# A convolution-attention and feed-forward kernel on one core: both instruction lists in a new order, and a result bank opened by whichever unit comes first

## The chip, the core and the metric

The kernel runs on one core of a Trainium2 chip. The time is device microseconds of one execution, here the median of three runs. The engines named are TensorE (PE, matrix products), VectorE (DVE), ScalarE (ACT), GpSimd (POOL) and SyncE (SP, which issues the transfers). Each works through its own list of instructions strictly in order and waits where an instruction needs something that is not there yet.

## What is computed

A softmax over seven taps weighs seven shifted copies of `x`; the result goes through a feed-forward layer with a gate.

```
w = softmax(weight_gen, axis=-1)            # B=4, S=4096, H=8, K=7 taps
x_unf = x_pad[:, idx, :].reshape(B, S, K, H, 24)
x = einsum('bshk,bskhg->bshg', w, x_unf)    # -> 16384 tokens x 192
h = x @ w_in                                # 192 -> 2048
g = h * (1.0 / (1.0 + exp(-1.702 * h)))
out = g @ w_out                             # 2048 -> 192
```

## The kernel before

**Tiling.** The 16,384 tokens are cut into 32 blocks of 512, and the 2048 hidden columns into 16 groups of 128. One block with one group is a unit; there are 512. Block 0 is computed in fp32, the others in fp16 with each number split into a high and a low part, so that three products stand in for one.

**Per unit, from block 3 on.** `pair` (L661, `P.k` in the lists) makes the first products of two units in two banks, 18 matmuls on 64-row halves of the array. The gate of a unit is a tanh on ACT (L595, `gt`) and a multiply on DVE (L600, `gm`); then ACT writes the high part of `g` (L613, `gh`) and DVE the low part (L615, `gl`). Only `gl` frees the bank. Unit n uses bank h(n mod 4), so a pair waits for the `gl` of the two units two pairs earlier. `upper` (L677, `U.n`, six matmuls) adds the unit to 128 of the 192 output columns in two PSUM banks; `lower` (L690, `C.b`, 48 matmuls) does the remaining 64 columns for a whole block at once, and two small matmuls of a later block follow it (L351, `top`).

**Per block, the attention.** `softmax` has seven steps (`s`): maximum (DVE), subtraction (POOL L210), exp and sum, a small constant (ACT L220), reciprocal (DVE L222), multiply (POOL L228). `attend` then does seven taps (POOL L244) and six additions (POOL L260) on 128x768. `scales` takes the largest magnitude (DVE L369, L341, L346), spreads it with `top`, and makes powers of two of it (DVE L357 to L363); `cg` (L379) and `co` (L384) derive two more numbers from them. ACT then rounds the tile to its high part (L420, `x.0`), and DVE makes the low part in two instructions (L423, `x.1` with 128x512 and `x.2` with 128x256), both of whose inputs lie in SBUF. SP transposes the parts (L429, `tu`) and copies halves of them (L438/L441, `xd`); pairs need both. SP also loads weights and `x` for two blocks at a time (L199, L186, `lp`), and stores results after ACT and DVE have scaled them (`stU`, `stV`, `stLa`, `stLb`).

**What sets the order.** Every engine's order comes from two written lists of steps. `ORDER` has 923 items, for the start up to block 7 or so; `PERIOD` has 246, two blocks or 32 units, and is repeated with the block and unit numbers moved on by two blocks and 32 units. `act` walks them item by item, and each item issues its instructions on whatever engines it uses. No scheduler rearranges them. In a period the numbers are relative, so that `C.-1` is the `lower` of the block before (called the first place below) and `C.0` the next one's (the second place). Where the lists repeat, one period of the trace stands for all; the times below are from the one around 602 us.

**The start.** Block 0 is turned round by matmuls. Its columns beyond 128 (the rest) are built from seven partial products on POOL (L279), summed two by two (L314, `rests`) and transposed onto PE by L325 (`trb`). First products of block 0 are `W` and `X` (L567; L583, L584).

**Opening a bank.** In `upper` and `second` the first unit of a block, f = 0, allocates the result bank and sets `start`, and the last, f = 15, sets `stop`; so in the lists unit 0 is first and unit 15 last.

Of the kernel before, what the change touches and what calls it, by code (L numbers as in the profile page):

```python
# [22 lines left out]
P.0 a4.1 gh.-2 gm.-1 gl.-2 gh.-1 gl.-1 s1.2 U.-6 gt.0 a4p.1 P.1 gm.0 gt.1 gh.0 gm.1 gl.0 a5.1 U.-5 gt.2  # L23
stLb.-2 U.-4 gh.1 s0.3 gm.2 s2.2 U.-3 a5p.1 gl.1 gh.2 U.-2 s3.2 P.2 gl.2 s4.2 gt.3 a6.1 gm.3 co.-1 gh.3 s5.2
U.-1 gt.4 gl.3 a6p.1 U.0 stU.-1 gm.4 U.1 gt.5 stV.-1 P.3 s6.2 c0.1 a0.2 gm.5 C.-1 gt.6 a1.2 gh.4 gm.6 gt.7
gl.4 gh.5 gm.7 a1p.2 gh.6 gh.7 gl.6 gl.7 s1.3 gl.5 a2.2 P.4 c2.1 x0.1 a2p.2 s2.3 U.2 gt.8 P.5 x1.1 gt.9
stLa.-1 a3.2 gm.8 gh.8 gm.9 U.3 gh.9 U.4 x2.1 gt.10 a3p.2 gl.9 U.5 tu.1 gt.11 gl.8 U.6 gm.10 P.6 gh.10 gm.11
a4.2 gl.10 gh.11 gl.11 U.7 gt.12 a4p.2 U.8 gm.12 gt.13 xd.1 P.7 gh.12 gm.13 lp.4 gl.12 a5.2 co.0 cg.1
stLb.-1 U.9 gt.14 U.10 a5p.2 gh.13 gm.14 U.11 gl.13 gh.14 U.12 gt.15 P.8 a6.2 gm.15 gl.14 gh.15 s3.3 gl.15
a6p.2 U.13 gt.16 U.14 gm.16 gt.17 P.9 gh.16 gm.17 gl.16 gh.17 gl.17 U.15 gt.18 c0.2 P.10 stU.0 gt.19 stV.0  # L30
gm.18 U.16 gh.18 gm.19 C.0 gh.19 s4.3 gt.20 gm.20 gl.19 gh.20 gl.18 gt.21 gl.20 gm.21 gh.21 P.11 c2.2 stLa.0
# [12 lines left out]
nm.o2 n2.t1 s2.1 n1.o2 a1.4p nm.o4 W.8 na.i2w n2.o2 S.3 gm.6 gt.7 s3.1 s2.2 W.9 gm.7 a1.5 nm.o3 s2.3 S.4
n1.o3 s2.4 s3.2 na.i0w n2.o3 a1.5p X.2 s2.5 n1.o4 na.t0w s3.3 n2.o4 s2.6 bin.0 S.5 a1.6 gt.8 gt.9 gm.8
na.o2w gm.9 W.10 a1.6p s3.4 bin.1 W.12 gt.10 bin.2 na.o0w W.11 c1.0 a2.0 S.6 gt.11 nm.o5 gm.10 a2.1 ph.t0w
c1.1 W.13 c1.2 n1.o5 S.7 x1.0 pd.t0w a2.1p gm.11 n2.o5 X.3 na.o4w x1.1 a2.2 bout.0 S.8 gt.13 gt.12 s3.5
ph.i0w x1.2 bout.1 W.15 s3.6 gm.13 tu1 a2.2p bout.2 S.9 gt.15 gm.12 ph.o2w W.14 pl.i0w S.10 ph.o0w pl.t0w
ph.o4w xd1 W.16 pl.o2w S.11 gt.14 ps.o0w pl.o0w hold.B W.17 ph.i2w lp2 a2.3 gm.14 S.12 ps.o2w gm.15 cg1 X.4
pl.o4w S.13 gt.16 gt.17 a2.3p gm.16 W.18 gm.17 gh.16 gl.16 W.19 gt.18 a2.4 gh.17 W.20 gm.18 gt.19 gl.17  # L50
S.14b gh.18 gm.19 a2.4p S.14a gl.18 gh.19 W.21 co1 gl.19 S.15b a2.5 X.5 S.15a gt.21 pl.i2w W.22 st.0a gt.20
S.16a a2.5p gm.21 st.0b W.23 gm.20 gh.21 S.16b gh.20 gl.21 S.17a gt.22 a2.6 gl.20 S.17b gt.23 gm.22 W.24
gm.23 gh.22 a2.6p W.25 gh.23 gl.22 ps.o4w S.18 gl.23 s5.0 a3.0 c2.0 X.6 S.19 gt.24 gt.25 gm.24 W.27 a3.1
gm.25 gh.24 c2.1 S.20 c2.2 gh.25 gt.27 a3.1p gl.25 W.26 x2.0 s4.0 gm.27 S.21 gt.26 gl.24 a3.2 gh.27 W.29
gm.26 gh.26 S.22 x2.1 W.28 s4.1 cg2 gl.26 a3.2p s4.2 S.23 gl.27 X.7 S.24 gt.28 x2.2 a3.3 gt.29 tu2 gm.28
W.30 s4.3 gh.28 gm.29 S.25 gt.30 a3.3p co2 gm.30 W.31 gl.28 gh.30 S.26 gh.29 a3.4 gt.31 gl.29 xd2 mv W.32
gm.31 W.33 a3.4p gl.30 gh.31 S.27 gl.31 X.8 a3.5 S.28 gt.33 gt.32 gm.33 W.34 a3.5p s4.4 gm.32 gh.33 S.29
gh.32 gl.33 gt.34 s4.5 W.35 gl.32 a3.6 gm.34 S.30a gt.35 W.36 gh.34 gm.35 s4.6 S.30b gl.34 a3.6p gh.35 W.37
gl.35 S.31a X.9 c3.0 st.1a a4.0 S.31b gt.36 W.38 st.1b gm.36 gt.37 s5.1 S.32b gh.36 a4.1 gm.37 W.39 gt.38
gl.36 S.32a s5.2 gm.38 gh.37 S.33b a4.1p gh.38 c3.1 S.33a c3.2 gt.39 W.40 gl.37 x3.0 S.34 gm.39 a4.2 co3  # L60
gh.39 gl.38 W.41 s5.3 gl.39 a4.2p S.35 X.10 S.36 gt.41 x3.1 gt.40 a4.3 gm.41 W.43 gm.40 S.37 gt.43 x3.2
gh.41 W.42 a4.3p tu3 gh.40 S.38 gl.40 gt.42 gl.41 W.44 a4.4 gm.42 gm.43 S.39 gh.42 gh.43 gl.42 a4.4p W.45
s5.4 cg3 gl.43 xd3 S.40 a4.5 lp3 a4.5p X.11 S.41 gt.44 a4.6 gt.45 W.46 gm.45 S.42 gm.44 a4.6p gh.45 gt.46
gl.45 W.47 gh.44 gm.46 S.43 gl.44 gh.46 c4.0 gt.47 P.24 gm.47 s6.0 gl.46 S.44 gt.48 s7.0 gh.47 gm.48 c4.1
gt.49 S.45 gl.47 gh.48 gm.49 P.25 c4.2 gh.49 gl.48 x4.0 gl.49 U.48 gt.50 P.26 gm.50 gt.51 s5.5 gh.50 x4.1
s5.6 gm.51 S.46b S.46a gl.50 a5.0 gh.51 S.47b gt.52 gl.51 S.47a gt.53 gm.52 U.49 a5.1 st.2a gm.53 P.27 gh.52
gh.53 hold.A x4.2 gl.52 a5.1p tu4 U.50 gl.53 gt.54 U.51 cg4 gm.54 gt.55 P.28 a5.2 gh.54 gm.55 gh.55 st.2b
gl.55 a5.2p U.52 gt.56 gl.54 U.53 xd4 gt.57 gm.56 U.54 gh.56 gm.57 s6.1 P.29 gh.57 hold.C a5.3 gl.57 gl.56
U.55 gt.58 a5.3p P.30 gm.58 gt.59 gh.58 gm.59 gl.58 a5.4 gh.59 U.56 gt.60 gl.59 U.57 gt.61 gm.60 P.31 a5.4p
gh.60 gm.61 gh.61 gl.61 U.58 a5.5 gt.62 gl.60 U.59 gt.63 gm.62 P.32 gh.62 gm.63 a5.5p gl.62 gh.63 gl.63 U.60  # L70
gt.64 a5.6 U.61 gm.64 gt.65 P.33 gh.64 gm.65 a5.6p gl.64 gh.65 gl.65 U.64 gt.66 U.62 gm.66 gt.67 P.34 gh.66
gm.67 s6.2 gl.66 gh.67 gl.67 U.63 gt.68 c5.0 P.35 stU.3 gt.69 gm.68 stV.3 U.65 gt.70 gm.69 C.3 gh.68 gt.71
gl.68 gh.69 s6.3 gm.70 gl.69 gh.70 s6.4 s6.5 gl.70 s6.6 gm.71 a6.0 P.36 c5.2 a6.1 cg5 x5.0 gh.71 x5.1 U.66
gt.72 U.67 gl.71 a6.1p gt.73 U.68 gm.72 P.37 gh.72 gm.73 x5.2 gh.73 a6.2 tu5 gl.73 lp4 U.69 gl.72 gt.74 U.70
gm.74 gt.75 a6.2p P.38 co4 gh.74 gm.75 gl.74 gh.75 a6.3 gl.75 U.71 gt.76 xd5 P.39 gm.76 gt.77 a6.3p gh.76
gm.77 stLa.3 U.72 gh.77 s7.1 U.73 gl.77 a6.4 s7.2 U.74 gl.76 gt.78 s7.3 U.75 gm.78 gt.79 U.76 s7.4 a6.4p
gh.78 s7.5 P.40 gm.79 s8.0 gh.79 gl.78 a6.5 gl.79 U.77 gt.80 stLb.3 P.41 gm.80 gt.81 a6.5p gh.80 gm.81 gl.80
gh.81 U.78 gt.82 gl.81 U.79 a6.6 gt.83 gm.82 P.42 gh.82 gm.83 gl.82 a6.6p gh.83 stU.4 gl.83 U.80 gt.84 stV.4
P.43 gt.85 s7.6 c6.0 a7.0 gm.84 C.4 gt.86 a7.1 gh.84 gl.84 a7.1p gm.85 gh.85 gm.86 gl.85 gh.86 a7.2 gt.87
gm.87 U.81 c6.2 gh.87 s8.1 P.44 gl.86 x6.0 a7.2p cg6 gl.87 s8.2 U.82 x6.1 gt.88 P.45 stLa.4 gm.88 a7.3 gt.89  # L80
gh.88 gm.89 U.83 x6.2 gh.89 co5 a7.3p tu6 U.84 gt.90 gl.88 gl.89 U.85 gt.91 gm.90 U.86 a7.4 gh.90 gm.91 P.46
gl.90 gh.91 gl.91 a7.4p U.87 gt.92 xd6 U.88 gm.92 gt.93 P.47 a7.5 gh.92 gm.93 gl.92 gh.93 gl.93 U.89 a7.5p
gt.94 U.90 gm.94 U.91 s8.3 gh.94 P.48 a7.6 gt.95 gl.94 gm.95 gh.95 a7.6p U.92 gt.96 gl.95 U.93 gm.96 gt.97
# [900 lines left out]
```

## Time and profile before

| | |
|---|---|
| median of 3 runs | 1048.82 us (1048.38 to 1048.83) |
| profiled execution, its span | 1046.4 us |
| profiled execution, its own time | 1048.8 us, 2.4 us more than its span |
| PE | 1037.9 us busy, 9238 matmuls |
| DVE | 865.2 us busy, 1577 instructions |
| ACT | 717.9 us busy, 1210 instructions |
| POOL | 733.5 us busy, 502 instructions |
| granted PE clock | 9 tenths or more in all 40 slices |

The profile is of one execution. Matmuls overlap, so a PE busy time is read from the starts of the instructions rather than from their lengths. A bracket at the end of a row gives the idle time of the engine ahead of that instruction and what ended it. A row of several equal instructions (x2) gives the time from the first start to the last end.

### The profile page before, as it was taken

What the parts mean: (1) busy time and instruction counts of PE and PEld (TensorE: products, weight loads), DVE (VectorE), ACT (ScalarE), POOL (GpSimd) and SP (SyncE); (2) the same over time, 40 slices, a digit from 0 to 9 for tenths busy, and PEclk for the clock granted to TensorE, in tenths of its full rate; (3) what the DMA queues carried; (4) which work ended last, traced back from release to release, by engine and by line L of the source; (5) the groups of instructions that cost most, each with busy time, mean ns of one, the idle gap of its engine ahead of it and who ended that gap; (6) DMA issues with size and microseconds to landing.
All of it is one profiled execution on the core that took longest, in us unless ns stands there. A gap on an engine that the chain in (4) does not pass through costs nothing.

```text
span 1046.4 us, 23146 instructions
## 1 busy us (share of the span) xinstructions
PE 1037.9 (99%) x9238; PEld 506.3 (48%) x9238; DVE 865.2 (83%) x1577; ACT 717.9 (69%) x1210; POOL 733.5 (70%) x502
## 2 busy tenths in 40 slices
...
GB/s 351 48 81 54 93 46 102 32 36 103 47 95 48 40 81 46 98 47 81 50 35 108 36 103 47 32 93 47 98 47 60 58 47 108 36 42 31 36 42 21
DMA packets 70948, 70.81 MB, mean 68 GB/s; under 512 B 52092, under 2 KB 57596, under 8 KB 69432
## 3 DMA queue, kind: packets, MB, share of 16 engines
...
q10 hardware_dynamic: 144, 0.13, 0.0%
...
## 4 chain that ended last, share of the span: by engine, by line
PE 87%; DVE 5%; DMA 2%; POOL 2%; issue 2%; ACT 1%; SPq 0%; ACTq 0%; POOLq 0%
PE h L661 39%; PE o L677 24%; PE o L690 14%; PE o L626 2%; DVE h L600 2%; DVE xs L423 2%; PE h L567 1%; POOL acc L260 1%; PE o L629 1%; ACT th L595 1%; DVE g L615 1%; PE o L631 1%; PE o L630 1%; POOL prod L244 1%; DMA ro<-in_moe_w_out_dram 1%
## 5 line engine op out<-in xcount | busy, mean ns | idle before, releaser
L595 ACT ACTIVATE th<-h,s 128x512 f32<-128x512 f32 x496 | 323.3, 684 | 128.9 <-PE h L661 112.8
L600 DVE SCALAR_TENSOR_TENSOR h<-th,h 128x512 f32<-128x512 f32 x496 | 328.7, 691 | 99.5 <-ACT th L595 99.3
L260 POOL TENSOR_TENSOR acc<-acc,prod 128x768 f32<-128x768 f32 x186 | 344.6, 1853 | 12.9
L244 POOL TENSOR_TENSOR prod<-xb,wb 128x768 f32<-128x768 f32 x186 | 288.9, 1553 | 10.9
L661 PE MATMUL h<-xt,w0h 64*128 64x512 f16 x928 | 199.4, 376 | 0.0
L613 ACT ACTIVATE g<-h 128x512 f16<-128x512 f32 x228 | 134.9, 597 | 65.9 <-DVE h L600 65.5
L228 POOL TENSOR_TENSOR wb<-wb,wr 128x224 f32<-128x224 f32 x31 | 18.1, 584 | 206.8 <-DVE wr L222 204.3
L661 PE MATMUL h<-xt,th 64*128 64x512 f16 x464 | 160.5, 376 | 0.0
L615 DVE SCALAR_TENSOR_TENSOR g<-g,h 128x512 f16<-128x512 f16 x228 | 149.2, 680 | 13.4 <-ACT g L613 9.0
L661 PE MATMUL h<-xd,rt 64*128 64x512 f16 x720 | 153.5, 376 | 0.4 <-DMA xd<-xt 0.4
L661 PE MATMUL h<-rt 64*128 64x512 f16 x672 | 138.9, 376 | 0.0
L661 PEld LDWEIGHTS <-rt 64*128 64x128 f16 x1392 | 90.4, 94 | 73.8 <-issue 0.2
L613 ACT ACTIVATE ro<-h 128x512 f16<-128x512 f32 x164 | 96.3, 597 | 38.4 <-DVE h L600 38.2
L615 DVE SCALAR_TENSOR_TENSOR ro<-ro,h 128x512 f16<-128x512 f16 x164 | 107.4, 681 | 9.6 <-ACT ro L613 6.2
L661 PE MATMUL h<-xt,w0l 64*128 64x512 f16 x464 | 109.5, 378 | 2.5 <-DVE g L615 1.5
L661 PE MATMUL h<-xd,th 64*128 64x512 f16 x240 | 90.2, 376 | 0.0
L677 PE MATMUL o<-g,wos 64*128 64x512 f16 x392 | 89.3, 376 | 0.0
L677 PE MATMUL o<-g,woh 64*128 64x512 f16 x392 | 89.3, 376 | 0.0
L677 PE MATMUL o<-g,wol 64*128 64x512 f16 x392 | 89.3, 376 | 0.0
L661 PEld LDWEIGHTS <-w0h 64*128 64x128 f16 x928 | 61.4, 94 | 55.3 <-issue 0.6
L661 PEld LDWEIGHTS <-th 64*128 64x128 f16 x928 | 61.5, 94 | 54.7
L661 PE MATMUL h<-xt,tl 64*128 64x512 f16 x232 | 87.2, 376 | 0.0
...
## 6 DMA issues: line engine op xcount, KB each, us to landing
...
```

What stands on the lines that cost most here:

```text
L228: eng.tensor_tensor(w, w, r, ALU.mult)
L244: eng.tensor_tensor(to.rearrange("p j (h g) -> p (j h) g", g=G), xv, wv, ALU.mult)
L260: nc.gpsimd.tensor_tensor(acc, acc, t, ALU.add)
L423: nc.vector.scalar_tensor_tensor(t[:, :, to : to + n], a[:, :, c : c + n], s, t[:, :, c : c + n], ALU.mult, ALU.subtract)
L595: nc.scalar.activation(t, hp[u], AF.Tanh, scale=scale[u[0]][:, 4:5] if u[0] else SIG / 2)
L600: nc.vector.scalar_tensor_tensor(to, th.pop(u), 1.0, hp[u], ALU.add, ALU.mult)
L613: nc.scalar.activation(g[:, 0], hp[u], AF.Copy, scale=2.0**-12)
L615: nc.vector.scalar_tensor_tensor(g[:, 1], g[:, 0], -(2.0**12), hp.pop(u), ALU.mult, ALU.add)
L626: nc.tensor.matmul(o, lhsT=g[:, s], rhs=w, start=a and j % 2 == 0, stop=z, skip_group_check=True)
L661: nc.tensor.matmul(to, lhsT=w, rhs=x, start=i == 0, stop=i == last)
L677: nc.tensor.matmul(po[blk, e], lhsT=w[h, f * D : f * D + P], rhs=g[h, i], start=f == 0 and i == 1, stop=w is woh and f == NF - (5 if blk = ...
L690: nc.tensor.matmul(po[blk, 2][h * C1 : (h + 1) * C1], lhsT=w[:, d + P : d + D], rhs=gg[blk, f + h][:, i], start=f == 0 and i == 1, stop=f ...
```

## The change

Both lists are written in another order. No item is added or removed. In `second` and `upper` the first unit to come, whichever it is, now opens the bank, and the last to come closes it; a dictionary `summed` counts them.

```diff
-    hp, th, gg, po, osb = {}, {}, {}, {}, {}
+    hp, th, gg, po, osb, summed = {}, {}, {}, {}, {}, {}
@@ second
-        a, z = f == 0, f == NF - 1
+        seen = summed.setdefault((blk, j), [])
+        seen.append(f)
+        a, z = len(seen) == 1, len(seen) == NF
@@ upper
-        if f == 0:
+        seen = summed.setdefault(blk, [])
+        seen.append(f)
+        first, n = len(seen) == 1, len(seen)
+        if first:
             for e in range(2):
                 po[blk, e] = seat(blk, e)
...
-                    start=f == 0 and i == 1, stop=w is woh and f == NF - (5 if blk == NB - 1 and e else 1),
+                    start=first and i == 1, stop=w is woh and n == NF - (4 if blk == NB - 1 and e else 0),
@@ PERIOD (one line of each)
-cg.2 x0.2 s5.3 gl.21 s6.3 x1.2 U.17 gt.22 P.12 a0.3 gm.22 gt.23 gh.22 gm.23 x2.2 gh.23 U.18 a1.3 gl.22 gt.24
+gt.20 gm.21 gh.21 gm.20 gl.18 gh.19 gl.19 c2.2 s6.3 lp.5 gh.20 gl.20 a0.3 P.11 gl.21 x0.2 x1.2 a1.3 U.20 gt.22
@@ ORDER (one line of each)
-n2.i0 tb.5p s1.3 trb.2 ka.0 ka.1 nm.t0 tb.6 s1.4 W.0 s1.5 nm.i1 n1.t0 s1.6 W.2 nb.i1 tb.6p n2.t0 trb.4 n1.i1
+n2.i0 s1.2 s1.3 s1.4 ka.1 tb.6 n1.t0 s1.5 n2.t0 nb.i1 trb.2 ka.0 tb.6p W.0 trb.4 nm.i1 kb.3 kb.1 kb.2 n1.i1 W.2
```

In the changed kernel the lines ahead of `second` stand three lines earlier. DVE at the second place of a period, from the gate behind `lower` to the one behind the second low part, before (L222 is the reciprocal, L423 the low parts):

```order
L600 SCALAR_TENSOR_TENSOR h<-th,h 128x512
L357 TENSOR_SCALAR s<-top 128x1
L361 TENSOR_SCALAR s<-s 128x1
L362 TENSOR_SCALAR s<-s 128x1
L363 TENSOR_SCALAR s<-s 128x1
L379 TENSOR_SCALAR s<-s,sc 128x1
L222 RECIPROCAL wr<-wm 128x32
L615 SCALAR_TENSOR_TENSOR g<-g,h 128x512
L423 SCALAR_TENSOR_TENSOR xs<-acc,s,xs 128x4x128
L600 SCALAR_TENSOR_TENSOR h<-th,h 128x512 x2
L423 SCALAR_TENSOR_TENSOR xs<-acc,s,xs 128x4x64
L615 SCALAR_TENSOR_TENSOR g<-g,h 128x512 x2
```

The same stretch after (L219 is the reciprocal, L597 the gate, L612 the split, L420 the low parts):

```order
L219 RECIPROCAL wr<-wm 128x32
L597 SCALAR_TENSOR_TENSOR h<-th,h 128x512 x2
L612 SCALAR_TENSOR_TENSOR g<-g,h 128x512 x2
L354 TENSOR_SCALAR s<-top 128x1
L358 TENSOR_SCALAR s<-s 128x1
L359 TENSOR_SCALAR s<-s 128x1
L360 TENSOR_SCALAR s<-s 128x1
L612 SCALAR_TENSOR_TENSOR g<-g,h 128x512 x2
L420 SCALAR_TENSOR_TENSOR xs<-acc,s,xs 128x4x128
L597 SCALAR_TENSOR_TENSOR h<-th,h 128x512 x2
L420 SCALAR_TENSOR_TENSOR xs<-acc,s,xs 128x4x64
L612 SCALAR_TENSOR_TENSOR g<-g,h 128x512 x2
```

The reciprocal, on which POOL's next block waits, moved ahead of two gates, two splits and the scale's numbers; `cg` (L379) moved behind the stretch, and one more split stands ahead of the first low part. On PE, the work between `lower` and the second pair behind the next one is still two pairs and four `upper`.

SP around the transpose of block 5, from one store to the next, before (L429 is the transpose, L199 and L186 the loads of blocks 8 and 9, L441 the copies `xd`):

```order
L703 DMA out_dram<-osb 128x512
L429 DMA_TRANSPOSE xt<-xs 128x12x128
L199 DMA wb<-in_weight_gen_dram 128x448
L186 DMA xb<-in_x_dram 128x2688
L441 DMA xd<-xt 64x1536 x2
L733 DMA out_dram<-osb 64x512
```

And after:

```order
L705 DMA out_dram<-osb 128x512
L196 DMA wb<-in_weight_gen_dram 128x448
L183 DMA xb<-in_x_dram 128x2688
L426 DMA_TRANSPOSE xt<-xs 128x12x128
L438 DMA xd<-xt 64x1536 x2
L735 DMA out_dram<-osb 64x512
```

The two loads moved from between the transpose and the copies to ahead of the transpose.

POOL at the start, the last products of the rest and the first of block 1's attention, before:

```order
L279 TENSOR_TENSOR rest<-xb,x_109 128x288
L210 TENSOR_TENSOR wb<-wb,wm 128x224
L279 TENSOR_TENSOR rest<-xb,x_109 128x288
L314 TENSOR_TENSOR rests<-rest 128x256
L279 TENSOR_TENSOR rest<-xb,x_109 128x288
L228 TENSOR_TENSOR wb<-wb,wr 128x224
L314 TENSOR_TENSOR rests<-rests,rest 128x256
L244 TENSOR_TENSOR acc<-xb,wb 128x768
```

And after:

```order
L207 TENSOR_TENSOR wb<-wb,wm 128x224
L276 TENSOR_TENSOR rest<-xb,x_109 128x288 x2
L311 TENSOR_TENSOR rests<-rest 128x256
L276 TENSOR_TENSOR rest<-xb,x_109 128x288
L311 TENSOR_TENSOR rests<-rests,rest 128x256
L225 TENSOR_TENSOR wb<-wb,wr 128x224
L241 TENSOR_TENSOR acc<-xb,wb 128x768
```

The last sum of the rests moved ahead of the multiply of block 1's softmax.

## Rows read from the trace of the kernel before

**Rows 1.** The page's first part: busy time, share of the span, instructions.

```profile
PE 1037.9 (99%) x9238; PEld 506.3 (48%) x9238; DVE 865.2 (83%) x1577; ACT 717.9 (69%) x1210; POOL 733.5 (70%) x502
```

**Rows 2.** Who waited for line L615 on DVE: us in total, times.

```profile
  PE h L661: 2.5, 12
```

**Rows 3.** Chain of waits, 598 to 617 us: start us, us, what.

```profile
599.53 1.94 PE h L661 x18
601.48 0.65 PE o L677 x6
...
607.43 2.09 PE h L661 x18
...
610.29 1.29 DVE h L600 x2
611.59 1.33 DVE xs L423
...
613.12 1.28 DVE g L615 x2
```

**Rows 4.** Timeline of PE, 602 to 615 us: start us, us, instruction.

```profile
602.05 0.41 PE L690 MATMUL o<-ro,wos 128*64 128x512 f16 x2
...
613.85 0.39 PE L661 MATMUL h<-xt,w0l 64*128 64x512 f16 x1
614.44 0.39 PE L661 MATMUL h<-xt,w0l 64*128 64x512 f16 x1 [0.21 <-DVE g L615]
```

**Rows 5.** Timeline of DVE, 571 to 614 us.

```profile
571.75 0.94 DVE L369 TENSOR_REDUCE top<-acc 128x1 f32<-128x768 f32 x1
...
573.07 0.69 DVE L600 SCALAR_TENSOR_TENSOR h<-th,h 128x512 f32<-128x512 f32 x1
...
608.40 0.34 DVE L222 RECIPROCAL wr<-wm 128x32 f32<-128x32 f32 x1
...
609.20 0.81 DVE L423 SCALAR_TENSOR_TENSOR xs<-acc,s,xs 128x512 f16<-128x512 f32 x1
...
611.49 1.70 DVE L423 SCALAR_TENSOR_TENSOR xs<-acc,s,xs 128x256 f16<-128x256 f32 x1
```

**Rows 6.** Timeline of POOL, 569 to 613 us.

```profile
569.73 0.58 POOL L228 TENSOR_TENSOR wb<-wb,wr 128x224 f32<-128x224 f32 x1 [0.26 <-DVE wr L222]
...
571.89 1.54 POOL L244 TENSOR_TENSOR prod<-xb,wb 128x768 f32<-128x768 f32 x1
573.51 1.81 POOL L260 TENSOR_TENSOR acc<-acc,prod 128x768 f32<-128x768 f32 x1
...
608.88 0.58 POOL L228 TENSOR_TENSOR wb<-wb,wr 128x224 f32<-128x224 f32 x1 [15.20 <-DVE wr L222]
609.54 1.87 POOL L244 TENSOR_TENSOR acc<-xb,wb 128x768 f32<-128x768 f32 x1
611.37 1.54 POOL L244 TENSOR_TENSOR prod<-xb,wb 128x768 f32<-128x768 f32 x1
```

**Rows 7.** Timeline of all engines at 171 us.

```profile
171.07 0.48 DVE L423 SCALAR_TENSOR_TENSOR xs<-acc,s,xs 128x256 f16<-128x256 f32 x1
171.12 1.84 POOL L244 TENSOR_TENSOR prod<-xb,wb 128x768 f32<-128x768 f32 x1
```

**Rows 8.** Timeline of ACT at 609 us.

```profile
609.57 1.27 ACT L595 ACTIVATE th<-h,s 128x512 f32<-128x512 f32 x2 [0.46 <-PE h L661]
```

**Rows 9.** Timeline of PE at 182 us.

```profile
182.80 0.37 PE L661 MATMUL h<-xd,rt 64*128 64x512 f16 x1 [0.37 <-DMA xd<-xt]
```

**Rows 10.** Timeline of POOL and PE, 15 to 19 us.

```profile
15.38 0.57 POOL L228 TENSOR_TENSOR wb<-wb,wr 128x224 f32<-128x224 f32 x1 [0.57 <-DVE wr L222]
15.92 0.72 POOL L314 TENSOR_TENSOR rests<-rests,rest 128x256 f32<-128x256 f32 x1
...
18.77 0.70 PE L583 MATMUL h<-x,rt 64*128 64x512 f32 x1 [0.50 <-ACT x L412]
```

**Rows 11.** Busy us by engine, 20 to 30 us (count), then clock, DMA share, GB/s.

```profile
20.00:30.00 10.00, 10.00 (x39) 5.49 (x36) 9.34 (x17) 9.93 (x16) 9.61 (x6) 1.00 0.78 264
```

More of the change, by code (lines that the diff above doesn't have):

```diff
@@ L22 @@
 PERIOD = """
[L23 to L31, printed above, removed]
-cg.2 x0.2 s5.3 gl.21 s6.3 x1.2 U.17 gt.22 P.12 a0.3 gm.22 gt.23 gh.22 gm.23 x2.2 gh.23 U.18 a1.3 gl.22 gt.24
@@ L33 @@
-tu.2 U.19 gl.23 gt.25 U.20 gm.24 a1p.3 P.13 gh.24 gm.25 gl.24 gh.25 gl.25 a2.3 U.21 gt.26 P.14 xd.2 gm.26
-gt.27 s0.4 lp.5 gh.26 a2p.3 gm.27 gl.26 gh.27 U.22 gt.28 gl.27 U.23 a3.3 gt.29 gm.28 P.15 gh.28 gm.29 gl.28
-gh.29 a3p.3 gl.29 U.24 gt.30 U.25 gm.30 gt.31
+s0.3 U.-5 U.-6 a4.1 a4p.1 gh.-2 gm.-1 s1.2 gh.-1 gl.-2 P.0 s2.2 gt.1 gl.-1 stLb.-2 gm.1 U.-4 gt.0 s3.2 gm.0 P.1
+s1.3 gh.1 co.-1 gh.0 gt.2 gl.1 gt.3 gl.0 gm.2 U.-2 a5.1 gh.2 s4.2 a5p.1 U.-3 U.-1 gm.3 gl.2 gh.3 gl.3 a6.1 P.2
+U.0 a6p.1 c0.1 stU.-1 P.3 gt.5 stV.-1 gt.4 gm.5 gm.4 s5.2 C.-1 gh.5 gl.5 gt.6 gt.7 gm.7 s6.2 gh.4 gm.6 gl.4 gh.7
@@ new lines @@
+a0.2 a1.2 gh.6 U.5 s2.3 gl.6 c2.1 x0.1 gl.7 stLa.-1 x1.1 a1p.2 a2.2 P.4 gt.9 a2p.2 P.5 gm.9 cg.1 lp.4 a3.2 gt.8
+gh.9 gt.10 gm.8 a3p.2 x2.1 gl.9 gm.10 gh.8 U.4 U.2 a4.2 U.6 U.3 gh.10 gt.11 gl.8 U.1 gm.11 gl.10 gh.11 P.6 U.10
+a4p.2 tu.1 gt.13 gt.12 xd.1 gl.11 P.7 s3.3 stLb.-1 gm.13 U.8 a5.2 gh.13 U.11 gm.12 gl.13 gh.12 U.13 gt.15 gt.14
+gl.12 P.8 gm.15 gm.14 gh.15 gl.15 gh.14 U.7 gt.16 U.12 co.0 s4.3 gl.14 a5p.2 U.9 gt.17 U.14 U.15 gm.16 gh.16
+gm.17 gh.17 stU.0 gl.16 gl.17 stV.0 P.9 a6.2 gt.19 gt.18 a6p.2 gm.18 U.16 c0.2 P.10 gt.21 gh.18 C.0 gm.19 s5.3
@@ L36 @@
+gt.20 gm.21 gh.21 gm.20 gl.18 gh.19 gl.19 c2.2 s6.3 lp.5 gh.20 gl.20 a0.3 P.11 gl.21 x0.2 x1.2 a1.3 U.20 gt.22
+P.12 gm.22 U.21 gt.23 gm.23 gh.22 x2.2 gl.22 a1p.3 gh.23 U.17 gl.23 U.19 gt.25 gt.24 P.13 U.23 gm.24 cg.2 gm.25
+gh.24 a2.3 gl.24 a2p.3 gh.25 gt.27 gl.25 U.18 gm.27 P.14 gt.26 U.22 U.24 gh.27 gm.26 tu.2 gh.26 s0.4 gl.27 gt.29
+gl.26 stLa.0 gm.29 gt.28 xd.2 P.15 gm.28 gh.29 a3.3 a3p.3 U.25 gh.28 gl.29 gl.28 gt.30 gm.30 gt.31
 """
 ORDER = """
-warm.15 s0.0 ident s0.1 s0.2 s0.3 s0.4 s0.5 s0.6 s0.7 ta.4 tb.0 ta.2 tb.1 tr.4 nm.i0 ta.6 tb.1p tr.2 nb.i0
@@ L39 @@
-ta.0 tb.2 nb.t0 ta.1 trb.0 tb.3 tr.6 ta.5 tb.3p ta.3 tr.5 tb.4 s1.0 sum.0.1 tr.3 s1.1 n1.i0 tr.0 tb.5 s1.2
-n2.i0 tb.5p s1.3 trb.2 ka.0 ka.1 nm.t0 tb.6 s1.4 W.0 s1.5 nm.i1 n1.t0 s1.6 W.2 nb.i1 tb.6p n2.t0 trb.4 n1.i1
-a1.0 W.1 kb.1 kb.3 kb.0 kb.2 nm.o0 n2.i1 X.0 a1.1 nb.o0w a1.1p n1.o0 W.3 gt.0 gt.1 gm.0 nm.o1 gm.1 W.4 a1.2
-gt.2 n2.o0 gt.3 W.5 n1.o1 nm.i2 gm.3 S.0a nb.i2w a1.2p gm.2 S.0b n2.o1 nb.t1 X.1 n1.i2 nm.i3 a1.3 nb.o2w
-n1.i3 n2.i2 S.1a a1.3p gt.5 s3.0 S.1b n2.i3 nm.t1 nb.o4w W.6 n1.t1 s2.0 a1.4 W.7 gm.5 gt.4 gt.6 S.2 gm.4
@@ L44 @@
[L44 to L83, printed above, removed]
@@ L84 @@
-P.49 gh.96 gm.97 stLb.4 gh.97 gl.96 U.94 gl.97 U.95 c7.0 U.96 stU.5 P.50 gt.98 stV.5 gt.99 gm.98 gh.98 gm.99
-C.5 gh.99 s8.4 gt.100 gm.100 gl.99 gh.100 gl.98 gt.101 gl.100 gm.101 gh.101 P.51 stLa.5 c7.2 cg7 x7.0 s8.5
-gl.101
+ident s0.0 s0.1 s0.2 s0.3 s0.4 s0.5 s0.6 s0.7 warm.15 tb.0 ta.4 nm.i0 tr.4 nb.t0 ta.6 ta.3 ta.0 tr.6 tb.1 tb.1p
+ta.5 tb.3 ta.2 tr.3 tb.2 s1.0 tb.3p trb.0 tr.5 ta.1 s1.1 tb.5 nm.t0 tb.4 nb.i0 sum.0.1 tr.2 tr.0 tb.5p n1.i0
+n2.i0 s1.2 s1.3 s1.4 ka.1 tb.6 n1.t0 s1.5 n2.t0 nb.i1 trb.2 ka.0 tb.6p W.0 trb.4 nm.i1 kb.3 kb.1 kb.2 n1.i1 W.2
@@ new lines @@
+nm.o0 kb.0 W.1 s1.6 a1.0 X.0 n2.i1 nb.o0w n1.o0 gt.0 a1.1 a1.1p gm.0 W.3 n2.o0 W.4 gt.1 nm.o1 gt.2 n1.o1 S.0a
+S.0b a1.2 gm.1 n2.o1 nb.t1 nm.i2 gm.2 gt.3 a1.2p gm.3 W.5 nb.i2w n1.i2 s2.0 n2.i2 nm.i3 s2.1 n1.i3 a1.3 X.1 gt.5
+gt.4 gm.5 gm.4 s3.0 W.6 nb.o2w a1.3p s3.1 n2.i3 nm.t1 n1.t1 W.7 W.9 n2.t1 nb.o4w a1.4 nm.o2 gt.6 S.2 n1.o2 S.1b
+s2.2 a1.4p nm.o4 W.8 gm.6 n2.o2 n1.o4 na.i2w n2.o4 gt.7 na.i0w a1.5 a1.5p nm.o3 gm.7 na.t0w n1.o3 s2.3 S.3 s2.4
+n2.o3 na.o2w S.6 s2.5 S.7 bin.0 X.2 s2.6 bin.1 W.10 gt.9 nm.o5 gm.9 bin.2 s3.2 gt.8 na.o0w S.5 gm.8 ph.t0w a1.6
```

39 lines of the change are left out of this document (added).

## The prediction

> **What bounds the kernel now.** I read the page first. TensorE (PE) is busy 99% of the span [rows 1] at granted clock 1.00 in every slice, VectorE (DVE) 83%, ScalarE 69%, GpSimd (POOL) 70%. No matmul is added or removed, so the time can only move by the idle time of PE, 8.5 us in all (1046.4 - 1037.9), and by new idle time. The question is which waits of PE make it up, which of them the new order takes away, and which it makes.
>
> The answer came from who waits for each line. DVE's L615 (`split`, which frees a first-product bank) holds PE up 12 times [rows 2]. That count is one per period of two blocks. The chain of waits shows the place [rows 3]: from `upper` through `lower` it lies on PE alone; after the pair that follows `lower` it leaves PE for two gates L600, one low part L423 and two L615, and only then returns. PE's own rows give the price [rows 4]: a pair (18 matmuls) takes 1.94 us, so two matmuls side by side are 0.215 apart, but P.13 starts at 613.85 and its second bank at 614.44, 0.59 later: 0.375 too much, 12 times, 4.5 us.
>
> DVE's rows name the guilty instruction [rows 5]: the second low part, 128x256, takes 1.70 us from 611.49, while twice that size, 128x512, took 0.81 at 609.20. POOL's rows say why [rows 6]: a tap began at 611.37, 0.12 ahead of it, and ends at 612.91; the low part ends 0.28 after that. In the first blocks the order of arrival is the other way round [rows 7]: the same low part begins at 171.07, the tap at 171.12, and now the low part takes 0.48 and the tap 1.84 instead of its 1.54. So of the two, the one that starts first runs through and the other waits: 1.22 us for DVE if it loses, 0.3 for POOL.
>
> By the Trainium skill ("SBUF — State Buffer", section "SBUF: two separate sides"), the port pair that DVE and GpSimd share is an exclusive lock, taken for a whole instruction by whichever starts first. The two places just read agree. The rule speaks against this change as well: a low part that comes hundredths late pays for a whole POOL instruction, and more for an add than for a tap. The sum below would be the same without the page; the losing case is the first rival.
>
> **The steady period.** Times are from S, the first matmul of `lower` at the second place (602.05 before). PE does the same work between `lower` and P.13 in both orders (two pairs, four `upper`), so P.13 is due at the same S+11.8 and the gate L600 of the pair after `lower` at the same S+8.24 (610.29), and the 128x256 low part comes up at the same S+9.44 (611.49). What moves is POOL. Its multiply L228 stood idle 15.20 us until DVE's reciprocal at 608.40, S+6.35 [rows 5, 6]. After, the reciprocal stands behind the scale's maximum (L369 and two more) and one gate, ahead of the splits. I walk there from PE. P.9 starts two pairs and one `upper` ahead of S: S-4.53. The first tanh comes 2.14 after the start of its pair (609.57 against 607.43 [rows 3, 8]): S-2.39; the unit that DVE takes first is the second in ScalarE's list, some 0.6 on, and its gate 0.72 behind its tanh (610.29 against 609.57): about S-1.1. One gate 0.60 (1.29 for two less 0.69 for one), the scale's group 1.32 (573.07 against 571.75), another gate 0.60: reciprocal at S+1.4, multiply 0.48 later (608.88 against 608.40) at M = S+1.9. This chain has perhaps 0.1 us of slack either way.
>
> From M POOL runs multiply, tap, tap, add: 573.51 + 1.81 - 569.73 = 5.59, so the add ends at S+7.5 [rows 6]. The 128x512 low part comes up at about S+7.4 (one split of 0.6 more ahead of it, two small instructions of 0.4 together less), waits those 0.1, and needs an estimated 0.55 behind the add's end (twice the 0.28 above): done at S+8.05, ahead of its next gate at S+8.24. The tap that it holds up is longer by 0.33, as at 609.54 (1.87 against 1.54 [rows 6]). It begins 0.08 after the add (571.89 + 1.54 to 573.51), and the next add a tap's pitch of 1.62 plus 0.33 later: M+7.62, S+9.5. The 128x256 low part comes up at S+9.44, in the 0.08 us between the two: it goes first, takes 0.48 instead of 1.70, and both splits end 1.22 us earlier, at 613.17 on the clock of before, 0.7 ahead of P.13. The stall goes: -4.5 us. The cover is thin: if M is 0.1 earlier, this turns into the first rival.
>
> At the first place (T, the first matmul of `lower` there) the reciprocal moves the other way, from ahead of `lower` to T+0.5, so M is about T+0.95. By the same POOL walk the add ends at T+6.5, the next tap at T+8.15; the 128x512 low part comes up at T+7.0 into that tap and ends at T+8.7, ahead of its gate (T+8.9). The add that it pushes back ends at T+10.4, the next tap starts 0.08 later, and the 128x256 low part comes up at T+10.2: served when the add ends, which costs 0.2. P.6, due at T+13.1, needs splits that are done by T+12.5. Nothing: 0.
>
> Elsewhere in the period, the shortest way from one pair to the next grows from three `upper` to four, 0.65 us more for a chain of tanh, gate, copy, split that needs about 3.4; that can only help. DVE, ScalarE and POOL do the same instructions; SP's loads go ahead of the transpose but end long before it. 0 for all of these.
>
> **The second-product flags.** Which unit opens a bank costs no instruction. It lets `upper` run in any order; 0, or it would show as new waits for stores.
>
> **Blocks 3 to 7.** PE waits once for the doubled copy `xd` at 182.80, 0.37 us [rows 9]; its DMA stands on SP behind two loads of block pair 4. After, those loads stand ahead of the transpose, so `xd` has the queue to itself: -0.4. Bounds: 0 if the loads themselves are still moving then, -0.5 if the neighbouring gaps go too.
>
> **The start.** POOL is idle 0.57 ahead of the multiply at 15.38, and the add of rests at 15.92 that PE waits for stands behind it [rows 10]. After, that add comes first. With the idle time and the multiply out of its way it can start near 14.9, so the transposes that wait for it run about 1 us earlier, and the first half-row pair X.0, which is at 18.77 and waits for ScalarE, comes near 17.9. That is -0.9 of PE's time there. PE then has less cover in the stretch where ScalarE is busy 9.93 and DVE 9.34 of 10 us [rows 11]; the front's list is otherwise wholly redrawn over 170 us. I take a third back: -0.6, bounds -0.9 and +1.0 (a new wait as long as the longest that PE has now).
>
> **Sum.** -4.5 - 0.4 - 0.6 = -5.5 on the profiled execution's span of 1046.4: 1040.9. Its own time is 2.4 us above its span, and is the median of the runs shown, so 1043.3.
>
> **Rivals.**
> First, the low part at the second place loses to the add (slower). For: a margin of under 0.1 us. Against: two chains that add up to the middle of the window. The add would start at S+9.43, end at S+11.24, the low part at S+11.5, the splits 1.27 later at S+12.8. Before they ended at 614.39, S+12.34. So P.13 is held 0.46 longer than now: +5.5 over 12 periods, -1.0 from the rest: 1053.3. It decides once POOL's multiply starts before about S+1.8. Chance 0.13.
>
> Second, the first place's 128x256 low part loses to the tap there (slower). It then waits a whole tap, the splits end at T+13.8, and P.6, due at T+13.1, stalls 0.7, 12 times: +8.4 - 5.5 = +2.9, 1051.7. For: the walk there rests on more instructions; against: 0.25 of slack, on the side of M later than T+0.7. Chance 0.10.
>
> Third, the change doesn't do what it says: the stall at P.13 stays as long (the low part still meets a tap, or PE then waits for ScalarE's copies at the same bank), and only the `xd` wait and the start are won: 1048.8 - 1.0 = 1047.8. For: only one of the instructions ahead of the split gets shorter. Chance 0.17.
>
> **How the numbers follow.** The forecast has 0.60: 1043.3. Its own range goes from 1041.5 (the start gives all 0.9, and some of PE's smaller waits go, up to 1 us) to 1046 (the start costs 1.0 and some of the 12 stalls stay). With the third case and half of the second, the range for 8 in 10 is 1041.5 to 1050. A measurement can tell about 0.2% here, 2.1 us. Faster than that: the forecast but for a tail, and a little of the third, 0.64; within it, most of the third and parts of the forecast's and the second's tails, 0.19; slower, the first and part of the second, 0.17.
>
> **What would show it.** Right: L423's 128x256 form at the second place near 0.5 us, with the add recorded right behind it at about S+9.5; the 12 waits of L661 for L615 gone and every second bank 0.22 behind the first; `xd` in no wait of PE; X.0 near 17.9. Wrong: the 128x256 form at 2 us there (first rival) or at the first place (second); a period as long as now (third); or new idle time of PE in 20 to 60 us above 1 us.

## The result and the profile after

The changed kernel takes 1039.62 us (median of 5 runs, 1039.20 to 1039.83) against 1048.72 for the kernel before (also 5 runs): ratio 0.9914, 95% interval 0.9902 to 0.9926. It is 9.1 us faster. The forecast was 5.5 us faster, 1043.3, with a range from 1041.5 to 1050; the direction held, the size did not. The profiled execution took 1039.64 us with a span of 1037.9.

The page's first part answers [rows 1]:

```profile
PE 1031.1 (99%) x9238; PEld 523.9 (50%) x9238; DVE 859.1 (83%) x1577; ACT 715.1 (69%) x1210; POOL 736.2 (71%) x502
```

PE still bounds. Its busy time fell by 6.8 us with the same 9238 matmuls, while its idle time (span less busy) went only from 8.5 to 6.8. So most of the gain was hidden in what the page counts as busy.

Who waited for the splits, now L612 (us in total, times), answers [rows 2]:

```profile
  PEld L660: 0.9, 5
```

The 12 waits of matmuls are gone. Weight loads (PEld), which waited for the splits 61 times before, 19.0 us in total, do so five times. The timelines of POOL and DVE at the second place answer [rows 5, 6]. S, the first matmul of `lower`, is 597.20 here:

```profile
599.13 0.58 POOL L225 TENSOR_TENSOR wb<-wb,wr 128x224 f32<-128x224 f32 x1 [6.76 <-DVE wr L219]
...
602.91 1.81 POOL L257 TENSOR_TENSOR acc<-acc,prod 128x768 f32<-128x768 f32 x1
604.79 1.87 POOL L241 TENSOR_TENSOR prod<-xb,wb 128x768 f32<-128x768 f32 x1
606.74 2.04 POOL L257 TENSOR_TENSOR acc<-acc,prod 128x768 f32<-128x768 f32 x1
```

```profile
598.63 0.35 DVE L219 RECIPROCAL wr<-wm 128x32 f32<-128x32 f32 x1
...
604.46 0.80 DVE L420 SCALAR_TENSOR_TENSOR xs<-acc,s,xs 128x512 f16<-128x512 f32 x1
...
606.64 0.48 DVE L420 SCALAR_TENSOR_TENSOR xs<-acc,s,xs 128x256 f16<-128x256 f32 x1
```

Against the walk: multiply at S+1.93 (1.9 predicted), the add's end at S+7.52 (7.5), the 128x256 low part at S+9.44 (9.44), the next add at S+9.54 (9.5). The low part comes up 0.10 ahead of that add and takes 0.48 instead of 1.70.

**Where the 8.5 us of span went.** The two traces can be compared where PE has done the same pairs, `upper` and `lower`. These are the starts of `lower` in us; at 222.40 the changed kernel has one `upper` less behind it, so 0.65 is added back in the difference there.

| `lower` of | before | after | difference |
|---|---|---|---|
| block 3 | 161.59 | 161.04 | -0.55 |
| block 4 | 193.03 | 191.71 | -1.32 |
| block 5 | 222.40 | 220.75 | -1.00 |
| block 7 | 285.63 | 284.01 | -1.62 |
| 22 blocks later | 981.55 | 973.01 | -8.54 |

The last 7 us are the repeated period: 696 us of it, at 63.23 us a period before and 62.62 after. The gain is 0.61 per period, not 0.375. Eleven periods at 0.61 make 6.7 of the 6.9 in the last two rows; the rest is small waits of single periods, the largest 0.16 at 493.33 before.

**The missing 0.23 us.** It lies at the other end of the period, where the prediction did not look. The first two steps of an undisturbed pair of the kernel before show what is normal:

```profile
599.37 0.38 PE L661 MATMUL h<-xt,w0l 64*128 64x512 f16 x2
599.58 0.38 PE L661 MATMUL h<-rt 64*128 64x512 f16 x2
```

A pair works in two halves of 64 rows, and a step is one matmul of each half. Two matmuls of 0.38 that together last 0.38 start together; the next step follows 0.215 later (1.94 for the nine steps of a pair). PE's timeline of the kernel before, ahead of the next `lower` (L690), 22 us after the stall in [rows 4]:

```profile
636.04 0.38 PE L661 MATMUL h<-xd,tl 64*128 64x512 f16 x1
636.04 0.38 PE L661 MATMUL h<-xt,th 64*128 64x512 f16 x1
636.25 0.38 PE L661 MATMUL h<-xd,th 64*128 64x512 f16 x1
636.56 0.41 PE L690 MATMUL o<-g,wos 128*64 128x512 f16 x2
```

The same place after (L692):

```profile
629.93 0.38 PE L660 MATMUL h<-xt,tl 64*128 64x512 f16 x1
629.93 0.38 PE L660 MATMUL h<-xd,tl 64*128 64x512 f16 x1
630.14 0.38 PE L660 MATMUL h<-xt,th 64*128 64x512 f16 x1
630.15 0.38 PE L660 MATMUL h<-xd,th 64*128 64x512 f16 x1
630.45 0.41 PE L692 MATMUL o<-g,wos 128*64 128x512 f16 x2
```

After, the two matmuls of the last step start together (630.14 and 630.15). Before, the tl step of one half (636.04) ran beside the last step of the other, and the last matmul of the late half ran alone, at 636.25. The halves had been a step apart ever since 614.44, when the late half's first matmul began. `lower` uses all 128 rows, so it had to wait for the late half.

This makes theory A: a second bank that is late by d costs PE d, of which what exceeds 0.215 is paid at once (the other half goes one step ahead and hides a step) and the rest at the next `lower`. Theory B: the step lost ahead of `lower` has a cause of its own, which the new order removes as well.

The Trainium skill ("TensorEngine Tiling (Array Packing)", section "Key Properties") says that tiles of the array work independently and that a change of the tiling mode drains the engine. The rows above agree with both: the halves are apart at 636.04, and the full-row matmul at 636.56 comes 0.31 behind the last one of the late half, 0.09 more than a step, as it does after (630.15 to 630.45).

### The profile page after: what moved, and what is told of

It reads as the page before. It is cut to its first block, busy times and chain, and to the rows that moved or that the text cites. A ratio compares the mean times of both kernels' runs of the same rounds, so it can differ in the third digit from the quotient of the medians.

```text
span 1037.9 us, 23035 instructions
## 1 busy us (share of the span) xinstructions
PE 1031.1 (99%) x9238; PEld 523.9 (50%) x9238; DVE 859.1 (83%) x1577; ACT 715.1 (69%) x1210; POOL 736.2 (71%) x502
## 4 chain that ended last, share of the span: by engine, by line
PE 97%; DVE 1%; DMA 1%; ACT 0%; SPq 0%; issue 0%; ACTq 0%
PE h L660 43%; PE o L679 29%; PE o L692 15%; PE o L625 2%; PE h L564 1%; PE o L628 1%; PE o L630 1%; PE o L629 1%; PE h L580 1%; PE h L569 1%; DMA wb<-in_weight_gen_dram 1%; PE h L572 1%; PE h L571 1%; PE h L570 1%; PE h L586 0%; DVE xs L420 0%
## 5 line engine op out<-in xcount | busy, mean ns | idle before, releaser
L597 DVE SCALAR_TENSOR_TENSOR h<-th,h 128x512 f32<-128x512 f32 x496 | 330.3, 690 | 106.1 <-ACT th L592 105.5
L660 PE MATMUL h<-xt,w0h 64*128 64x512 f16 x928 | 178.3, 376 | 0.0
L660 PE MATMUL h<-xt,th 64*128 64x512 f16 x464 | 174.0, 376 | 0.0
L612 DVE SCALAR_TENSOR_TENSOR g<-g,h 128x512 f16<-128x512 f16 x228 | 150.9, 682 | 6.8 <-ACT g L610 3.5
L660 PE MATMUL h<-xd,rt 64*128 64x512 f16 x720 | 138.3, 376 | 0.0
L225 POOL TENSOR_TENSOR wb<-wb,wr 128x224 f32<-128x224 f32 x31 | 17.9, 576 | 163.4 <-DVE wr L219 158.2
L612 DVE SCALAR_TENSOR_TENSOR ro<-ro,h 128x512 f16<-128x512 f16 x164 | 108.7, 680 | 3.8 <-ACT ro L610 0.8
L660 PEld LDWEIGHTS <-rt 64*128 64x128 f16 x1392 | 71.7, 94 | 75.9
L660 PE MATMUL h<-xt,w0l 64*128 64x512 f16 x464 | 89.6, 377 | 0.0
L660 PE MATMUL h<-rt,th 64*128 64x512 f16 x224 | 84.2, 376 | 0.0
L679 PE MATMUL o<-g,wos 64*128 64x512 f16 x392 | 76.0, 376 | 0.1
L679 PE MATMUL o<-g,woh 64*128 64x512 f16 x392 | 76.0, 376 | 0.0
L679 PE MATMUL o<-g,wol 64*128 64x512 f16 x392 | 76.0, 376 | 0.0
L610 ACT ACTIVATE ri<-h 128x512 f16<-128x512 f32 x104 | 61.3, 597 | 20.3 <-DVE h L597 19.4
```

The costliest lines, as they stand in the source:

```text
L225: eng.tensor_tensor(w, w, r, ALU.mult)
L597: nc.vector.scalar_tensor_tensor(to, th.pop(u), 1.0, hp[u], ALU.add, ALU.mult)
L610: nc.scalar.activation(g[:, 0], hp[u], AF.Copy, scale=2.0**-12)
L612: nc.vector.scalar_tensor_tensor(g[:, 1], g[:, 0], -(2.0**12), hp.pop(u), ALU.mult, ALU.add)
L660: nc.tensor.matmul(to, lhsT=w, rhs=x, start=i == 0, stop=i == last)
L679: nc.tensor.matmul(po[blk, e], lhsT=w[h, f * D : f * D + P], rhs=g[h, i], start=first and i == 1, stop=w is woh and n == NF - (4 if blk == ...
```

## The experiments

Each is shown by what differs from the kernel that its expectation names. Before and after were measured again beside them at 1048.4 to 1048.5 and 1039.62.

**e1: both halves wait together.**

```diff
-            for to, w, x in two:
+            for to, w, x in two[::-1]:
```

> The kernel before, with the two matmuls of each step of `pair` issued in the other order, so that the bank which is late at P.13 is the first one PE asks for, and both row halves wait together. Theory A (a pair's two halves run side by side, so a second bank late by 0.60 us costs 0.385 at once, when the first half runs a step ahead, and the other 0.215 at the next `lower`, which needs all rows and finds the halves a step apart): PE now loses 0.60 at once at P.13 and nothing at `lower`; the step of 0.21 between the last two matmuls ahead of `lower` is gone, the period stays 63.23, the time stays at 1048.7 within 0.5 us. Theory B (the 0.215 ahead of `lower` is a loss of its own, that the new order happens to remove as well): 0.60 at P.13 and still 0.215 at `lower`, period 63.45, 2.6 us slower.

Measured: 1050.63 us against 1048.44, ratio 1.0025 (1.0014 to 1.0035), a period of 63.44. The period is the one that B gave (63.45), but PE's rows show A's places. The stall at P.13, paid in full:

```profile
614.54 0.38 PE L677 MATMUL o<-g,woh 64*128 64x512 f16 x2
615.36 0.39 PE L661 MATMUL h<-xt,w0l 64*128 64x512 f16 x2 [0.43 <-DVE g L615]
...
620.98 0.38 PE L677 MATMUL o<-g,woh 64*128 64x512 f16 x2
621.32 0.39 PE L661 MATMUL h<-xt,w0l 64*128 64x512 f16 x2
...
637.38 0.38 PE L661 MATMUL h<-xd,th 64*128 64x512 f16 x1
637.39 0.38 PE L661 MATMUL h<-xt,th 64*128 64x512 f16 x1
637.69 0.41 PE L690 MATMUL o<-g,wos 128*64 128x512 f16 x2
```

From 614.54 to 615.36 is 0.82, 0.60 over a step. Ahead of `lower` (637.69) the halves start together, as after: nothing is lost there, so B is wrong. The added 0.2 us comes from two new small waits, 0.12 over a step at 620.98 (0.34 to the next row) and 0.075 at 631.47. Before, the late half was a step behind there and did not need its bank yet: the gap between the halves had covered those waits. My time for A left them out.

**e2: the reciprocal alone.** The constant's addition (`s4.3`) and the reciprocal (`s5.3`) of the second place are moved in the old period, nothing else.

```diff
-gm.18 U.16 gh.18 gm.19 C.0 gh.19 s4.3 gt.20 ...
-cg.2 x0.2 s5.3 gl.21 ...
+gm.18 U.16 s4.3 gh.18 gm.19 s5.3 C.0 gh.19 gt.20 ...
+cg.2 x0.2 gl.21 ...
```

> The kernel before, with only the constant's addition (ACT) and the reciprocal (DVE) of the second place moved: the reciprocal behind the second gate after the scale's maximum, some 6 us earlier, nothing else. By POOL's walk the multiply starts near S+0.7, the first low part waits for a tap and ends at S+8.4, the second waits for the add's end near S+10.1 and ends at S+10.4 instead of S+11.1; the splits then end 0.15 before P.13 is due, and the stall goes. Theory A: with it the 0.21 ahead of `lower` goes too, period 62.62, -7.3 us, 1041.4. Theory B: only the 0.385 goes, -4.6 us, 1044.1. If the low part ends later than S+10.6 a part of the stall is left.

Measured: 1042.78 against 1048.44, ratio 0.9946 (0.9934 to 0.9959): -5.7, between the times of A (1041.4) and B (1044.1). DVE's second low part waits for an add, but less long than before:

```profile
609.07 0.84 DVE L423 SCALAR_TENSOR_TENSOR xs<-acc,s,xs 128x256 f16<-128x256 f32 x1
```

It ends at 609.91, S+10.3 with S at 599.60. P.13 starts in step in 9 of the 12 periods (the first of the other three, at 233.98, keeps the whole stall of 0.60), and PE's rows show what is left, two pairs later and ahead of `lower`:

```profile
617.22 0.47 PE L661 MATMUL h<-xt,w0l 64*128 64x512 f16 x2
617.43 0.47 PE L661 MATMUL h<-rt 64*128 64x512 f16 x2
...
633.19 0.38 PE L661 MATMUL h<-xt,th 64*128 64x512 f16 x1
633.29 0.38 PE L661 MATMUL h<-xd,th 64*128 64x512 f16 x1
633.59 0.41 PE L690 MATMUL o<-g,wos 128*64 128x512 f16 x2
```

Two matmuls of 0.38 that together last 0.47: the second half is 0.09 late at 617.22, costs nothing there (the next step is 0.21 on), and the halves stay 0.10 apart until `lower`, which pays it. This is the small wait that e1 uncovered at 620.98: both fall on P.15, which has only three `upper` between itself and P.13, the pair whose banks it takes. Such a period takes 62.71, against 63.23 before and 62.62 after. So the moved reciprocal alone is worth some 0.52 of the 0.61, and the spacing of pairs by four `upper` is what can take the last 0.09; that part was not tried alone.

**e3: the reciprocal 0.6 us too early.**

```diff
-... gh.18 C.0 gm.19 s5.3
+... gh.18 C.0 s5.3 gm.19
```

> The changed kernel, with the reciprocal of the second place one instruction earlier, ahead of one gate instead of behind it (0.6 us). The rule of who starts first: POOL's tap then begins at S+7.0, ahead of the first low part (S+7.3), which waits for its end and is done at S+9.1 instead of 8.1; the second low part comes up at S+10.3, after the add has begun, waits for its end near S+10.75 and ends at S+11.0 instead of S+9.9; the second split ends at S+12.3, 0.5 after P.13 is due. Theory A prices that at its whole lateness, 0.5 x 12 = 6 us slower than the changed kernel (1045.6); theory B at 0.5 - 0.215 = 0.29 x 12 = 3.4 us (1043.0). If only an early reciprocal matters and not where POOL's instructions end: 1039.6, as the changed kernel.

Measured: 1043.83, ratio to before 0.9956 (0.9942 to 0.9969), 4.2 us slower than the changed kernel. POOL and DVE in the order of their starts:

```profile
605.66 1.54 POOL L241 TENSOR_TENSOR prod<-xb,wb 128x768 f32<-128x768 f32 x1
...
605.93 1.82 DVE L420 SCALAR_TENSOR_TENSOR xs<-acc,s,xs 128x512 f16<-128x512 f32 x1
...
607.28 2.14 POOL L257 TENSOR_TENSOR acc<-acc,prod 128x768 f32<-128x768 f32 x1
...
608.87 0.83 DVE L420 SCALAR_TENSOR_TENSOR xs<-acc,s,xs 128x256 f16<-128x256 f32 x1
```

With S at 598.67 the second low part ends at S+11.03 (11.0 expected). PE's price, at P.13 and ahead of `lower`:

```profile
610.47 0.88 PE L660 MATMUL h<-xt,w0l 64*128 64x512 f16 x2
610.96 0.60 PE L660 MATMUL h<-rt 64*128 64x512 f16 x2
...
632.12 0.38 PE L660 MATMUL h<-xd,th 64*128 64x512 f16 x1
632.42 0.41 PE L692 MATMUL o<-g,wos 128*64 128x512 f16 x2
```

0.49 from the first half's start to the second step, 0.28 over a step, and a last matmul alone ahead of `lower`, 0.21: 0.49 in all, for a half that is 0.49 late. The time alone lies nearer to B's 1043.0 than to A's 1045.6, but such a period takes 63.12 against 62.62, which is A's price. It happened in 8 of the 12 periods, and in a ninth, at 925 us, both banks were late and it cost 0.79: hence 4.2 us instead of 6. In one of the other three, POOL's tap began at 480.80, behind the first low part (480.20) instead of ahead of it, and the second took 0.57 from 482.38. Why POOL was later there was not looked into.

**e4: the loads ahead of the transpose.**

```diff
-... gh.73 a6.2 tu5 gl.73 lp4 U.69 ...
+... gh.73 a6.2 lp4 tu5 gl.73 U.69 ...
```

> The kernel before, with only the loads of blocks 8 and 9 ahead of the transpose of block 5 on SP. The wait of PE for the doubled copy near 182 us goes. Theory A: the second bank was late there by 0.74, so the next `lower` (193.03) comes 0.75 earlier, with no step of 0.2 ahead of it. As predicted before (0.37 by the bracket of the row): 0.4 earlier. If the loads themselves delay the copy: no change.

Measured: one time, 1048.36, which by itself can't be told from 1048.44; what follows rests on the trace. `lower` of block 4 starts at 192.27, 0.76 earlier than before, as A says: the row of [rows 9] hid a second half late by 0.74. But 0.58 of it is given back before the next `lower`, at a pair whose second bank is late too, which PE's wait for the copy had hidden before:

```profile
205.36 0.38 PE L661 MATMUL h<-xt,w0l 64*128 64x512 f16 x1
205.93 0.39 PE L661 MATMUL h<-xt,w0l 64*128 64x512 f16 x1 [0.20 <-DVE g L615]
```

The net is -0.18.

**e5 and e6: each list alone.** e5 is the changed kernel with the old `ORDER`, e6 with the old `PERIOD`.

```diff
-ORDER = """ ... after ... """
+ORDER = """ ... before ... """
```

> The changed kernel with the start's list of before: only the repeated period is new. Theory A (a late second bank costs its whole lateness; 12 stalls of 0.60 and three small skews of 0.1 to 0.16 go): -7.5 us, 1040.9, with every period at 62.62 and PE's blocks up to 160 us as before. The price that the prediction gave a stall (0.375): -4.5, 1043.9.

> The changed kernel with the period's list of before: only the start is new. Theory A: the 12 stalls stay at 0.60, the start gives 0.5 to 1.0 and the transposing DMA's order 0.75 less what a later wait takes back (0.3 by the trace after): -1.0, 1047.4. If the start gave much of the whole gain: -3 or more.

Measured: e5 1041.98, ratio 0.9936 (0.9922 to 0.9951), -6.4; e6 1046.76, ratio 0.9984 (0.9974 to 0.9993), -1.6. In e5 the periods take 62.62: from block 7 on, each one gains 0.61 on the kernel before, which prices the stall at A's 0.60. It missed my 7.5 because at the seam of the two lists, at 233.79, PE waits 0.54 once for something new and still pays one stall of 0.60, so only 11 of the 12 go. In e6 eleven stalls, from 295 us on, are as before: 0.60 to the second step and a lone matmul ahead of `lower`. In this execution the start gives more than I took for it, 0.94 by block 3 and 1.39 by block 5.

**e7: the start's copies first.** Two places of the changed kernel's start are moved.

```diff
-n2.i0 s1.2 s1.3 s1.4 ka.1 tb.6 n1.t0 s1.5 n2.t0 nb.i1 trb.2 ka.0 tb.6p W.0
+n2.i0 ka.0 ka.1 s1.2 s1.3 s1.4 tb.6 n1.t0 s1.5 n2.t0 nb.i1 trb.2 tb.6p W.0
-... a7.3p s8.3 gl.88 gt.90 gt.91 gl.89 U.86
+... a7.3p gl.88 gt.90 gt.91 gl.89 s8.3 U.86
```

> The changed kernel with two places of its start moved: ScalarE's and VectorE's copies of the turned tile ahead of block 1's softmax sum (PE waits 1.29 us for them at 15.95), and one softmax sum behind two splits near 203 (PE waits 0.27 there). If PE bounds the start all through: X.0 comes 1.1 us earlier, and with the 0.27 the time falls by 1.3, to 1038.3. If ScalarE and VectorE bound 20 to 60 us: X.0 comes earlier, PE waits as much more later, and only the 0.27 is left: 1039.3.

Measured: 1039.15, ratio 0.9910 (0.9896 to 0.9925), not told apart from the changed kernel's 0.9914. The second place gained nothing: PE still waits there, 0.28 over a step at 203.23. X.0 comes at 18.62, against 19.32 in the profile after and 18.90 in e3, which has the same start, and at block 3 PE is 0.3 ahead of e6, which has the same start as the changed kernel; by block 5 it is level again, since a second bank is 0.34 late at 206.96.

**e8 and e9: the changed kernel again, and the copies with an exchange.** e9 has e7's first edit, `U.82` and `U.88` exchanged, and `s8.3` behind `gl.91`.

> The changed kernel itself, once more, as the measure for the next one on the same chip, and to see how much the start's first transposes move between executions (PE waits 0.7 us for them at 6.56 in the profile after, not at all in two runs of the same start): 1039.2 to 1039.9.

> The changed kernel with the two copies of the turned tile ahead of block 1's softmax sum, and near 203 us two `upper` exchanged (unit 82 in the place of unit 88, which PE waits 0.28 for) and the softmax sum behind four splits instead of ahead of two. The copies alone gave 0.3 by 160 us and lost it again at 206.96, where a second bank was late by 0.34. If the exchange covers that wait: 0.5 less than the changed kernel by block 5 and in all. If the banks that the next pair waits for are late whatever runs ahead of it: no gain, within 0.2.

Measured: e8 1039.62 (1039.56 to 1039.79), e9 1038.94 (1038.58 to 1039.34); to before 0.9915 (0.9901 to 0.9929) and 0.9909 (0.9895 to 0.9923). Their runs don't overlap, but the intervals do: 0.7 us is at the edge of what can be told. The exchange itself gained nothing: against before, both kernels win the same 0.46 between block 3 and block 5, since in e9 a pair then waits for its bank (0.29 at 207.11). What e9 has, it has by block 3, at 160.74; but e3 and e6, without the copies' edit, are there at 160.63 and 160.65, and the profile after and e8 at 161.04 and 161.16. It is therefore not shown that the copies gained anything. e8's start shows a 0.41 wait at 7.27 for a tap that the profile after shows with 0.7 and e3 and e7 not at all, so part of a start's time differs between executions.

## Why the prediction was wrong

**What held.** The bound (PE), the guilty instruction, the rule of who starts first, the count of 12 and both walks: at the first place T is 630.45, and the two low parts start at T+7.05 and T+10.24 (7.0 and 10.2 predicted). Only the 0.2 that the second was to lose there did not come: it took 0.48. The new spacing, the flags and the added port conflicts cost nothing, as said; no rival came. e3 brought the first one about: its mechanism was the text's, at the instants that e3's own expectation gave (the second low part done at S+11.03 against 11.0).

```profile
637.50 1.67 DVE L420 SCALAR_TENSOR_TENSOR xs<-acc,s,xs 128x512 f16<-128x512 f32 x1 [0.27 <-ACT xs L417]
...
640.69 0.48 DVE L420 SCALAR_TENSOR_TENSOR xs<-acc,s,xs 128x256 f16<-128x256 f32 x1
```

**The step that failed** is the price of the stall: "two matmuls side by side are 0.215 apart ... 0.375 too much, 12 times, 4.5 us". Two matmuls side by side are 0.00 apart; it is the steps of two that are 0.215 apart. P.13's second bank was late by the whole 0.60 (0.59 between the rounded rows), not by 0.375. 18 matmuls in 1.94 us give only the step; how far apart the two of a step start is read from a row x2 of any undisturbed pair. So the 0.375 was what PE loses at once, and the other 0.21 at `lower` was left out. The premise went with it: "the time can only move by the idle time of PE, 8.5 us in all" leaves no room for that 0.21, and 6.8 of the 8.5 us that the span fell by were in what counts as busy (that both are 8.5 is chance). Nor did the sign "every second bank 0.22 behind the first" show; after, it is 0.00 behind. The term is 12 x 0.61 = 7.3. That is 2.8 of the 3.0 us by which the span missed. The time missed by 3.7: it lies 1.7 above the span here, where the forecast took over the 2.4 of before. The cause of this 0.7 stays open (later executions of before and after have 2.1 and 1.8). The measured price of a late second half, in us, over the normal steps:

| kernel, place | late by | paid at once | paid at `lower` |
|---|---|---|---|
| before, P.13 (613.85) | 0.60 | 0.39 | 0.21 |
| before, block 4 (182.06) | 0.74 | 0.53 | 0.20 |
| e4 (205.36) | 0.57 | 0.36 | 0.21 |
| e3, P.13 (610.47) | 0.49 | 0.28 | 0.21 |
| e2 (617.22) | 0.09 | 0 | 0.10 |
| e1, P.13, both halves (615.36) | 0.60 | 0.60 | 0 |

Five sizes of delay, two causes (a split, a DMA) and one reversal give the same rule.

**The copy `xd`** was undersized for the same reason (0.4, in truth 0.77 by block 4), and the give-back of 0.32 by block 5 was not foreseen; by chance the two nearly cancel, and -0.45 stands against -0.4. That is luck. e4 shows the pattern with a larger give-back.

**The start** was put at -0.6 and gave -0.55 by block 3 in this execution (-0.43 in e8, -0.96 in e3), in other ways than said, so this agreement is luck as well. X.0 came at 19.32, not 17.9: the waits at [rows 10] went, and a longer one came.

```profile
15.95 1.13 PE L564 MATMUL h<-x,ri 128*128 128x512 f32 x2 [1.29 <-ACT x L400]
...
19.32 0.70 PE L580 MATMUL h<-x,rt 64*128 64x512 f32 x1
19.33 0.70 PE L581 MATMUL h<-x,rt 64*128 64x512 f32 x1
```

The copy on ACT stood behind DVE's copy of the other half, which the new list puts behind block 1's softmax sum. Between 20 and 161 us PE then won back 1.1. One part is visible above: the two half-row matmuls now start together, where before the second came 0.45 after the first (18.77 and 19.22). The rest was not taken apart.

**The range** began at 1041.5 since all of its width below the forecast lay in the start and in smaller waits, and none in the price of a known stall, which I took for exact.
